# Attention tiled by head pairs and query halves, q and k in rows of 2 KB, v sums copied by DMA, and attention of batch 1 run before the experts

## The chip, the core and the metric

The kernel runs on one core of a Trainium2 chip. The time is device microseconds of one launch; the median of three runs stands for a kernel. The profile is one execution on the chip. Its engines are PE (matrix multiply, with PEld for its weight loads), DVE, ACT, POOL and SP; POOL and SP also issue the DMAs here (POOL those that load from DRAM and cast float32 to bf16, SP the rest).

## What is computed

Sparse attention over 4 batches, 8 heads, 768 positions of 64, followed by one expert (two matrix products) that is chosen for each batch from the mean over its positions. Cut to what matters:

```
k_sum = k.reshape(B, H, 24, 32, D).max(axis=3)      # 24 blocks of 32 keys
v_sum = v.reshape(B, H, 24, 32, D).mean(axis=3)
scores_l = scale * q @ k.T,  kept where |i - j| < 16, else -1e9
scores_s = scale * q @ k_sum.T + log(32)
a = softmax(concatenate([scores_l, scores_s]))
x = a @ concatenate([v, v_sum])                      # B, S, H * D = 512
e = argmax(x.mean(axis=1) @ w_gate)                  # one expert of 8 for each batch
out = gate_w * (relu(x @ w1[e]) @ w2[e])             # 512 -> 1024 -> 512
```

## The kernel before

Queries go in blocks of 64 (QB). A block's keys are 120 rows: its own 64, a halo of 16 on either side, and the 24 block maxima; `kaug` holds k transposed with these columns for each pair of heads and block, `vblk` the rows of v in the same order (own rows, halo rows R_PRE and R_POST, 24 rows of block sums). Four batches run one after another. Instructions are issued in the order in which the Python code calls them; nothing reorders them, and each engine works its own list in that order.

Loads: `load_k`, `load_q` (through `load_rows`, L83) issue six DMAs each, one for 128 positions of all heads, in rows of 256 bytes; `load_v` (L98) two DMAs, 256-byte rows too. All are in POOL's list. `halo` (L107) copies the halo rows of v inside `vblk` with SP DMAs once v has landed.

Attention of a batch: `T_k` (L191) transposes k on PE and copies it to `kaug`; `K_rest` (L206) adds halo columns and the maxima for the whole batch, on DVE; `V_sum` (L236) sums v by blocks on PE and copies the sums into `vblk` on DVE; then for each of six groups g of 128 queries, all heads at once: `T_q` (transpose q), `S_tile` (scores on PE, exponential on ACT, mask product on DVE), `O_tile` (product with v on PE, reciprocal and scaling on DVE), `X_tile` (transpose back on PE, copy on ACT, sum over positions on DVE, L346).

Expert of a batch: `gate` (L353) finds the expert and issues the six weight DMAs from POOL; `H_chunk` (L416) is one of 8 chunks of the first product, `O_chunk` (L438) half of one of six chunks of the second, with the scaling by the gate on ACT (L454) and an output DMA on SP (L455).

Order (L500 to L531): batch 0's attention alone; gate 0; loads of v and q of batch 1 behind the weights; k of batch 1; then `weave`, which puts steps of a second list between the items of a first: the first product of batch 0 with v and the first steps of q of batch 1, the second product with batch 1's S, O and X steps; and so on. After batch 3's gate, the rest of batch 2's second product and batch 3's expert run alone.

Of the kernel before, what the change touches and what calls it, by code (L numbers as in the profile page):

```python
# [22 lines left out]
def kernel(  # L23
# [71 lines left out]
    def load_q(b):
        load_rows(b, "q", q)

    def load_v(b):  # L98
        vb = vblks[b % NV]
        for a in range(2):  # L100
            hs = slice(4 * a, 4 * a + 4)
            nc.gpsimd.dma_start(  # L102
                vb[0:QB, hs, :, 0:D].rearrange("p h j d -> p (h j) d"),
                v[b, hs].rearrange("h (j p) d -> p (h j) d", p=QB),
            )

    def halo(b):  # L107
        vb = vblks[b % NV]
        for a in range(2):
            hs = slice(4 * a, 4 * a + 4)  # L110
            nc.sync.dma_start(
                vb[R_PRE : R_PRE + HALO, hs, 1:NJ, :],
                vb[QB - HALO : QB, hs, 0 : NJ - 1, :],
            )
            nc.sync.dma_start(
                vb[R_POST : R_POST + HALO, hs, 0 : NJ - 1, :], vb[0:HALO, hs, 1:NJ, :]
            )


    load_k(0)  # L120
    identb = const.tile([128, 128], BF16, name="identb")
    make_identity(nc, identb)
    it_u = const.tile([R_SUM, QB], I32, name="it_u")
    nc.gpsimd.iota(it_u, pattern=[[-1, QB]], base=0, channel_multiplier=1)
    it_p = const.tile([128, 1], I32, name="it_p")
    nc.gpsimd.iota(it_p, pattern=[[0, 1]], base=0, channel_multiplier=1)
    it_b = const.tile([QB, NJ, BLK], I32, name="it_b")
    nc.gpsimd.iota(it_b, pattern=[[-2, NJ], [1, BLK]], base=0, channel_multiplier=0)
    load_v(0)
    load_q(0)  # L130

# [3 lines left out]
    def edges(i):  # L135

        nc.vector.memset(vblks[i][0:QB, :, :, D:DP], 1.0)
        nc.vector.memset(vblks[i][QB:R_SUM, :, 0:1, :], 0.0)
# [34 lines left out]
    u_f = const.tile([R_SUM, QB], FP32, name="u_f")  # L173
    nc.vector.tensor_scalar(
        out=u_f, in0=it_u, scalar1=lo[:, 0:1], scalar2=None, op0=ALU.subtract
    )
    u_hi = const.tile([R_SUM, QB], FP32, name="u_hi")
    nc.vector.tensor_scalar(
        out=u_hi, in0=u_f, scalar1=float(2 * HALO - 2), scalar2=None, op0=ALU.is_le
    )  # L180
    mask = const.tile([NR, QB], BF16, name="mask")
    nc.vector.memset(mask[R_SUM:NR, :], 1.0)
    nc.vector.scalar_tensor_tensor(
        out=mask[0:R_SUM, :], in0=u_f, scalar=0.0, in1=u_hi, op0=ALU.is_ge, op1=ALU.mult
    )
    mask_b = mask.unsqueeze(1).to_broadcast([NR, 2 * H, QB])
# [4 lines left out]
    def T_k(b, gg):  # L191
        def f():
            k_nat = nat["k", b]
            ps = tps_pool.tile([128, NP, 2, 128], BF16, name="kps", tag="tps")
            for u in range(2):
                for pr in range(NP):
                    nc.tensor.transpose(  # L197
                        ps[:, pr, u, :], k_nat[:, 2 * gg + u, 2 * pr : 2 * pr + 2, :], identb
                    )
            nc.vector.tensor_copy(  # L200
                kaugs[b % 2][:, :, 4 * gg : 4 * gg + 4, 0:QB],
                ps.rearrange("p r u (t s) -> p r (u t) s", s=QB),
            )
        return f

    def K_rest(b):  # L206
        def f():
            ka = kaugs[b % 2]
            nc.vector.tensor_copy(
                ka[:, :, 1:NJ, R_PRE:R_POST], ka[:, :, 0 : NJ - 1, QB - HALO : QB]  # L210
            )
# [9 lines left out]
            cur = t1.rearrange("p n t s -> p (n t) s")  # L221
            while w > 1:
                w //= 2
                nxt = small.tile([128, NP * NB, w], BF16, name=f"t_{w}")
                nc.vector.tensor_tensor(
                    out=nxt, in0=cur[:, :, 0:w], in1=cur[:, :, w : 2 * w], op=ALU.max
                )
                cur = nxt
            kmx = cur.rearrange("p (r n) o -> p r (n o)", r=NP)
            nc.vector.tensor_copy(  # L230
                ka[:, :, :, R_SUM:NR],
                kmx.unsqueeze(2).to_broadcast([128, NP, NJ, NB]),
            )
# [101 lines left out]
    def X_tile(b, g):  # L335
        def f():
# [5 lines left out]
            for pr in range(NP):  # L342
                nc.tensor.transpose(xps[:, pr, 0, :], xs[:, pr, :, :], identb)  # L343
# [218 lines left out]
```

## Time and profile before

| | before |
|---|---|
| runs, us | 230.15, 228.45, 230.1 (median 230.1) |
| profiled execution, us | 228.99 |
| its span, us | 227.3 |
| PE busy | 151.1 us, 66% |
| DVE busy | 103.5 us, 46% |
| ACT busy | 81.8 us, 36% |
| POOL busy (mostly DMA issue) | 72.5 us, 32% |
| DMA packets | 92,578, of which 76,176 under 512 bytes |

The profiled execution's own time is 1.7 us longer than its span. A busy share is an average over stages with different limits; the stages are told apart by windows of the trace. The column PEclk of a window is the clock that the throttle granted to PE, as a share of full speed. A row `start us, us, what` of the chain of work that ended last says what the end of the program hung on at that time.

### The profile page before, as it was taken

Reading aid. Unit: us, or ns where it says so; the run is one execution under the profiler, and the core shown is the slowest. Engines: PE = TensorE matmul, PEld = TensorE weight load, DVE = VectorE, ACT = ScalarE, POOL = GpSimd, SP = SyncE. Lnnn points to the kernel's source line nnn. Section 1 sums busy time; section 2 is a strip of 40 time slices with the busy share of each in tenths; the row PEclk is TensorE's granted clock in tenths of the full one; section 3 lists DMA queues with packets and bytes.
Section 4 is the critical chain, followed back from the end, with each engine's and each line's share of the span. In section 5 each row is a group of like instructions: output and inputs, shape, how many; then the busy total and the mean of one; then the engine's idle time right before and its main releaser. Section 6 shows DMA issues by size and latency. Waiting matters only on the chain.

```text
span 227.3 us, 4141 instructions
## 1 busy us (share of the span) xinstructions
PE 151.1 (66%) x1721; PEld 90.8 (40%) x1736; DVE 103.5 (46%) x240; ACT 81.8 (36%) x113; POOL 72.5 (32%) x89
## 2 busy tenths in 40 slices
PE   0324596456029999822933999950899984999991
PEld 0213474432025555511612555520566552456440
DVE  2685689681006066750360626771167797100000
ACT  2000365102002666630420266650155684155441
POOL 7996100099335000009834684005100000520000
PEclk9999999999656999995895599995599999699998
DMA  7999990089999912219999999997990111399342
GB/s 46 120 135 140 138 50 0 0 105 194 166 133 140 118 46 95 92 50 111 185 168 134 139 136 149 200 198 109 152 169 0 49 49 46 41 185 237 66 165 94
DMA packets 92578, 25.88 MB, mean 114 GB/s; under 512 B 76176, under 2 KB 89488, under 8 KB 92560
## 3 DMA queue, kind: packets, MB, share of 16 engines
q0 software_dynamic: 87296, 17.83, 129.3%
q1 hardware_dynamic: 5264, 7.80, 12.8%
q8 instruction: 13, 0.21, 0.4%
q14 instruction: 5, 0.04, 0.1%
HBM read 35.67 MB, written 6.29 MB: 185 GB/s over the span
## 4 chain that ended last, share of the span: by engine, by line
PE 30%; DMA 29%; DVE 15%; ACT 8%; issue 8%; POOL 6%; POOLq 2%; SPq 0%; ACTq 0%
DMA vblk<-in_v_dram 18%; PE hps L424 12%; PE ops L445 11%; DMA w_sb<-in_moe_w_dram 8%; DVE aT L300 4%; DVE xs L327 4%; ACT aT L294 4%; DMA vblk<-vblk 4%; DVE red L346 3%; ACT o_sb L454 2%; POOL k_nat L87 2%; POOL vblk L102 2%; PE vsps L243 2%; PE ops L316 2%; POOL w_sb L383 1%
## 5 line engine op out<-in xcount | busy, mean ns | idle before, releaser
L424 PE MATMUL hps<-xT,w_sb 128*128 128x384 bf16 x256 | 54.2, 371 | 15.0 <-DMA w_sb<-in_moe_w_dram 14.9
L431 ACT ACTIVATE hT<-hps 128x768 bf16<-128x768 f32 x32 | 26.0, 811 | 72.0 <-PE hps L424 72.0
L445 PE MATMUL ops<-w_sb,hT 128*128 128x512 bf16 x177 | 47.0, 391 | 2.4 <-issue 0.8
L383 POOL DMA_DIRECT2D w_sb<-in_moe_w_dram x16 | 11.9, 758 | 104.1 <-DVE grec L397 82.4
L424 PEld LDWEIGHTS <-w_sb 128*128 128x128 bf16 x256 | 26.8, 109 | 35.4 <-DMA w_sb<-in_moe_w_dram 15.7
L294 ACT ACTIVATE aT<-sc 128x1024 bf16<-128x1024 f32 x24 | 24.5, 1021 | 26.7 <-PE sc L284 26.6
L87 POOL DMA_DIRECT2D k_nat<-in_k_dram x24 | 21.3, 898 | 14.5 <-DMA vblk<-in_v_dram 11.7
L300 DVE TENSOR_TENSOR aT<-aT,mask 120x1024 bf16<-120x1024 bf16 x24 | 16.6, 690 | 20.3 <-ACT aT L294 20.2
L445 PEld LDWEIGHTS <-hT 128*128 128x128 bf16 x192 | 17.3, 99 | 18.6 <-issue 2.9
L87 POOL DMA_DIRECT2D q_nat<-in_q_dram x24 | 21.4, 927 | 7.6 <-DMA w_sb<-in_moe_w_dram 6.6
L454 ACT ACTIVATE o_sb<-ops,gcol 128x512 f32<-128x512 f32 x24 | 16.5, 687 | 18.7 <-PE ops L445 17.0
L243 PE MATMUL vsps<-vblk,bind 64*32 64x132 bf16 x192 | 6.2, 286 | 24.3 <-DMA vblk<-in_v_dram 24.3
L345 ACT COPY xT<-xps 128x512 bf16<-128x512 bf16 x24 | 14.0, 585 | 13.8 <-PE xps L343 13.6
L200 DVE COPY kaug<-kps 128x1024 bf16<-128x1024 bf16 x12 | 8.1, 687 | 22.0 <-PE kps L197 22.0
L346 DVE TENSOR_REDUCE red<-xT 128x4 f32<-128x512 bf16 x24 | 16.3, 682 | 3.6 <-ACT xT L345 3.6
L327 DVE TENSOR_TENSOR xs<-ops,rv 128x512 bf16<-128x512 f32 x24 | 16.6, 692 | 0.8
L197 PE MATMUL kps<-identb,k_nat 128*128 128x128 bf16 x96 | 10.1, 275 | 10.1 <-POOL identb masks.py:199 7.4
L243 PEld LDWEIGHTS <-bind 64*32 64x32 bf16 x192 | 4.9, 126 | 26.3 <-issue 21.8
L316 PE MATMUL ops<-vblk,aT 120*64 120x65 bf16 x384 | 12.1, 210 | 3.9 <-DVE aT L300 1.6
L343 PE MATMUL xps<-identb,xs 128*128 128x128 bf16 x96 | 10.7, 241 | 4.5 <-DVE xs L327 4.5
L197 PEld LDWEIGHTS <-k_nat 128*128 128x128 bf16 x96 | 8.8, 127 | 11.5 <-DMA k_nat<-in_k_dram 5.5
L251 DVE CAST vs_sb<-vsps 128x132 bf16<-128x132 f32 x4 | 1.2, 293 | 26.5 <-PE vsps L243 26.5
(58 smaller groups left out, 132.8 us busy)
## 6 DMA issues: line engine op xcount, KB each, us to landing
out_dram<-o_sb SPq DMA_DIRECT2D x24, 256.0 KB, 2.0
w_sb<-in_moe_w_dram POOLq DMA_DIRECT2D x16, 256.0 KB, 6.4
w_sb<-in_moe_w_dram POOLq DMA_DIRECT2D x8, 512.0 KB, 10.6
k_nat<-in_k_dram POOLq DMA_DIRECT2D x24, 128.0 KB, 9.6
vblk<-in_v_dram POOLq DMA_DIRECT2D x8, 384.0 KB, 13.4
q_nat<-in_q_dram POOLq DMA_DIRECT2D x24, 128.0 KB, 13.4
vblk<-vblk SPq DMA_DIRECT2D x16, 90.8 KB, 8.4
wg_sb<-in_moe_w_gate_dram SPq DMA_DIRECT2D x1, 16.0 KB, 1.9
```

The source lines that it names most:

```text
L87: nc.gpsimd.dma_start(t[:, g, :, :], src[b, :, g * 128 : (g + 1) * 128, :].rearrange("h p d -> p h d"),)
L197: nc.tensor.transpose(ps[:, pr, u, :], k_nat[:, 2 * gg + u, 2 * pr : 2 * pr + 2, :], identb)
L243: nc.tensor.matmul(vs_ps[BLK * pr : BLK * (pr + 1), :], lhsT=bind[:, j, :], rhs=vb[0:QB, 2 * pr : 2 * pr + 2, j, :], start=(j == 0), stop= ...
L294: nc.scalar.activation(aT.rearrange("p n c -> p (n c)"), sc.rearrange("p h c -> p (h c)"), ACT.Exp, scale=SCALE,)
L300: nc.vector.tensor_tensor(out=aT[0:NR], in0=aT[0:NR], in1=mask_b, op=ALU.mult)
L316: nc.tensor.matmul(ops[w * QB : (w + 1) * QB, hh, pr, :], lhsT=aT[0:NR, hh, pr, w, :], rhs=vb[0:NR, 2 * pr + hh, 2 * g + w, 0 : D + 1], st ...
L327: nc.vector.tensor_tensor(out=xs.rearrange("p r h d -> p h r d"), in0=ops[:, :, :, 0:D], in1=rv.unsqueeze(3).to_broadcast([128, 2, NP, D]) ...
L346: nc.vector.tensor_reduce(out=red[b][:, :, g], in_=dst, axis=AX.X, op=ALU.add)
L424: nc.tensor.matmul(hps[:, half, 0:HB], lhsT=w1_sb[:, dt, ft * 128 : (ft + 1) * 128], rhs=xT[b][:, dt, half * HB : (half + 1) * HB], start= ...
L431: nc.scalar.activation(hTs[b][:, ft, :].rearrange("p (u s) -> p u s", u=2), hps[:, :, 0:HB], ACT.Relu,)
L445: nc.tensor.matmul(o_ps, lhsT=hTs[b][:, ft, st * 128 : (st + 1) * 128], rhs=w2_sb[:, ft, :], start=(ft == 0), stop=(ft == NFT - 1),)
L454: nc.scalar.activation(o_sb, o_ps, ACT.Copy, scale=gcols[b][:, 0:1])
```

## The change

q and k are loaded as `[96, heads, 512]`: eight neighbouring positions of a head lie in one partition, so a row of DRAM is 2 KB (512 float32) and a batch needs one DMA for k and one for q. In batch 0 the loads go pair of heads by pair of heads: k, v, q of heads 0 and 1, then of 2 and 3, and so on. The transposes are now 16 for each pair, 96 columns each, and the copies behind them (`T_k`, `T_q`) read PSUM with a step of 96 elements to bring positions back in order. q's copy is on ACT in batch 0.

Attention goes by pair of heads and half of the queries (u), six blocks of 64 each. `T_k` does all of a pair's columns: copy, two maxima, one reduce, halo columns, block maxima. The mask is added on PE in batch 0 (`mbias` times `ident6`, two matmuls of 384 columns for each S_tile) and multiplied on DVE in the others. The sum over positions comes from ACT's `accum_out` in `X_tile`. The copies of v's block sums into `vblk` are DMAs on SP, two for each pair, and the halos of batch 0 are issued by pair. Odd output chunks are scaled on DVE.

PSUM is cut into one score buffer of two banks, two for transposes and four single banks for all else. `H_chunk` is one half of the queries, so there are 16 of them.

Order: batch 0's attention, with batch 1's loads and masks in its middle; gate 0; the first 19 of 33 steps of batch 1's attention alone; then 9 H items of batch 0 woven with the other 14 steps; gate 1; 19 items of batch 0 with 22 of batch 2's 33 steps; 9 of batch 1 with the rest; gate 2; the same for batch 3; gate 3; the rest of batch 2; batch 3's expert. Weights of batch 0 come in five DMAs for w1, of the others in three, and two for w2.

```
+        nc.gpsimd.dma_start(
+            nat[which, b][:, h0:h1, :],
+            src[b, h0:h1].rearrange("h (p r) d -> p h (r d)", r=RR),
+        )
...
+    def transpose_pair(b, which, pr, name):
+        src = nat[which, b]
+        ps = tps_pool.tile([128, RR, PR], BF16, name=name, tag="tps")
+        for r in range(RR):
+            for hh in range(2):
+                nc.tensor.transpose(
+                    ps[hh * D : (hh + 1) * D, r, :],
+                    src[:, 2 * pr + hh, r * D : (r + 1) * D],
+                    identb[0:PR, 0:PR],
+                )
+        return ps
...
+    def T_k(b, pr):
+        def f():
+            ps = transpose_pair(b, "k", pr, "kps")
+            ka = kaugs[b % 2][:, pr]
             nc.vector.tensor_copy(
+                ka[:, :, 0:QB].rearrange("q j (p r) -> q j p r", r=RR),
+                ps.rearrange("q r (j p) -> q j p r", j=NJ),
+            )
...
+            nc.vector.tensor_reduce(
+                out=kmx, in_=t2.rearrange("p j t s -> p (j t) s"), axis=AX.X, op=ALU.max
+            )
...
+    def V_sum(b, prs):
...
+            for pr in prs:
+                for hh in range(2):
+                    nc.sync.dma_start(
+                        vb[R_SUM:NR, 2 * pr + hh, :, 0:D],
+                        vs_sb[BLK * pr : BLK * pr + NB, hh, :]
+                        .unsqueeze(1)
+                        .to_broadcast([NB, NJ, D]),
+                    )
...
+            nc.scalar.activation(
+                xT[b][:, pr, u * HB : (u + 1) * HB], xps, ACT.Copy,
+                accum_out=red[b][:, pr, u : u + 1],
+            )
...
+        for pr in range(p0, p1):
+            ahead = pre(pr + 1) if pr + 1 < NP else []
+            nq = [T_q(b, pr + 1)] if pr + 1 < NP else []
+            steps += [S_tile(b, pr, 0)]
+            steps += ahead[0:1]
+            steps += [S_tile(b, pr, 1)]
+            steps += ahead[1:]
+            steps += [O_tile(b, pr, 0), O_tile(b, pr, 1)]
+            steps += nq
+            steps += [X_tile(b, pr, 0), X_tile(b, pr, 1)]
...
+    a0 = attn(0, 0, NP)
+    run(a0[: len(a0) // 2])
     load_k(1)
     edges(1)
+    make_mask()
+    load_v(1, 0, 4)
+    load_v(1, 4, 8)
+    load_q(1)
+    run(a0[len(a0) // 2 :])
     gate(0)
     load_k(2)
+    a1 = attn(1, 0, NP)
+    n1 = len(attn(1, 0, 2))
+    run(a1[:n1])
+    m0, m1, m2, m3 = moe(0), moe(1), moe(2), moe(3)
+    weave(m0[0:9], a1[n1:])
...
+    weave(m0[9:28], a2[: 2 * len(a2) // 3])
+    weave(m1[0:9], a2[2 * len(a2) // 3 :])
...
+    weave(m1[9:28], a3[: 2 * len(a3) // 3])
+    weave(m2[0:9], a3[2 * len(a3) // 3 :])
     gate(3)
+    run(m2[9:])
+    run(m3)
```

POOL's list at the start of the program, before: k of batch 0 in six DMAs, the identity matrix and the index tables, v, q, k of batch 1, then what the gate waits for.

```order
L87 DMA k_nat<-in_k_dram 128x8x64 x6
masks.py:197 MEMSET identb 128x128
masks.py:199 ISA
masks.py:199 AFFINE_SELECT identb<-identb 128x128
L124 IOTA it_u 96x64
L126 IOTA it_p 128x1
L128 IOTA it_b 64x384
L102 DMA vblk_84<-in_v_dram 64x48x64 x2
L87 DMA q_nat<-in_q_dram 128x8x64 x6
L87 DMA k_nat<-in_k_dram 128x8x64 x6
L370 TENSOR_LOAD ix_601
```

The same place in the changed kernel, to the second pair's loads.

```order
L91 DMA k_nat<-in_k_dram 96x2x512
masks.py:197 MEMSET identb 128x128
masks.py:199 ISA
masks.py:199 AFFINE_SELECT identb<-identb 128x128
L104 DMA vblk_87<-in_v_dram 64x24x64
L91 DMA q_nat<-in_q_dram 96x2x512
L127 IOTA it_b 64x384
L129 IOTA it_p 128x1
L132 IOTA it_m 128x64
L133 IOTA it_m 128x16
L136 IOTA it_m 128x16
L91 DMA k_nat<-in_k_dram 96x2x512
```

The identity and the tables moved from behind six loads to behind one, and v and q of the first pair stand ahead of k of the second. Batch 1's loads now stand ahead of the gate's `TENSOR_LOAD`.

SP's list at the start, before: the gate weights, then the halo copies of batches 0 and 1 (two groups of four), then outputs.

```order
L133 DMA wg_sb<-in_moe_w_gate_dram 128x4x8
L111 DMA vblk_84<-vblk_84 16x4x726
L115 DMA vblk_84<-vblk_84 16x4x726
L111 DMA vblk_84<-vblk_84 16x4x726
L115 DMA vblk_84<-vblk_84 16x4x726
```

The same place in the changed kernel: for each pair two halos and two copies of block sums (`vs_sb`).

```order
L150 DMA wg_sb<-in_moe_w_gate_dram 128x4x8
L111 DMA vblk_87<-vblk_87 16x2x726
L115 DMA vblk_87<-vblk_87 16x2x726
L306 DMA vblk_87<-vs_sb 24x12x64 x2
L111 DMA vblk_87<-vblk_87 16x2x726
L115 DMA vblk_87<-vblk_87 16x2x726
L306 DMA vblk_87<-vs_sb 24x12x64 x2
```

The copies of block sums moved from DVE to this queue; a later pair's halo stands behind an earlier pair's copies.

ACT's list behind gate 0 (its exponential is `ex`), before: all eight chunks of batch 0's first product, then batch 1's first scores (`aT`) among the outputs.

```order
L393 ACTIVATE ex_624,se<-lg,negm 1x8
L431 ACTIVATE hT<-hps 128x768 x8
L294 ACTIVATE aT<-sc 128x1024
L454 ACTIVATE o_sb<-ops_866,gcol 128x512
L294 ACTIVATE aT<-sc 128x1024 x2
```

The same place in the changed kernel.

```order
L449 ACTIVATE ex_784,se<-lg,negm 1x8
L357 ACTIVATE aT<-sc 128x768 x2
L400 ACTIVATE xT,red<-xps 128x384 x2
L357 ACTIVATE aT<-sc 128x768 x2
L400 ACTIVATE xT,red<-xps 128x384 x2
L484 ACTIVATE hT<-hps 128x384
L357 ACTIVATE aT<-sc 128x768
L484 ACTIVATE hT<-hps 128x384
```

Two pairs of batch 1's attention (scores and transposes back) moved ahead of the first `hT`.

## Rows read from the trace of the kernel before

**Rows 1.** Windows by stage: stretch, length, busy us (count) by engine, PEclk, DMA, GB/s.

```profile
0.00:28.00 28.00, 8.38 (x132) 6.84 (x133) 16.39 (x40) 3.33 (x3) 20.05 (x29) 1.00 2.47 115
28.00:41.60 13.60, 10.19 (x188) 7.41 (x183) 11.61 (x24) 7.49 (x10) 0.00 (x0) 1.00 0.51 25
41.60:68.40 26.80, 10.69 (x99) 7.00 (x100) 8.34 (x26) 2.01 (x4) 14.62 (x17) 0.81 1.92 128
68.40:97.60 29.20, 27.41 (x327) 15.53 (x331) 16.67 (x33) 16.81 (x23) 3.13 (x4) 0.94 1.06 95
97.60:124.80 27.20, 11.97 (x125) 7.64 (x126) 7.72 (x21) 5.53 (x10) 14.73 (x17) 0.78 1.85 134
124.80:151.80 27.00, 24.96 (x309) 14.15 (x314) 16.78 (x34) 14.90 (x20) 11.10 (x12) 0.91 2.74 163
151.80:159.80 8.00, 0.37 (x9) 0.26 (x8) 2.24 (x9) 0.98 (x4) 4.04 (x6) 0.61 0.78 129
159.80:193.40 33.60, 28.52 (x399) 18.03 (x402) 22.84 (x48) 17.69 (x23) 0.43 (x1) 0.94 0.41 76
193.40:227.30 33.90, 28.61 (x144) 13.97 (x146) 0.90 (x7) 13.07 (x19) 4.45 (x6) 0.92 0.63 132
```

**Rows 2.** The chain that ended last: start us, us, what, count.

```profile
9.33 9.13 DMA vblk<-in_v_dram
...
19.11 8.66 DMA vblk<-vblk
...
51.38 15.44 DMA vblk<-in_v_dram
...
72.96 2.60 PE hps L424 x16
...
78.38 0.34 PE sc L284 x16
...
84.37 0.44 PE ops L316 x16
...
165.00 0.45 PE kps L197 x8
...
169.79 0.80 PE vsps L243 x48
...
213.03 9.67 PE ops L445 x44
```

**Rows 3.** Timeline, batch 0: start us, us, engine, line, instruction, count, idle before.

```profile
11.07 1.28 DVE L200 COPY kaug<-kps 128x1024 bf16<-128x1024 bf16 x2
...
23.94 0.61 PE L284 MATMUL sc<-qT,kaug 64*128 64x64 bf16 x16 [2.97 <-DVE qT L271]
```

**Rows 4.** Groups by line and shape: busy us, mean ns of one, idle before.

```profile
L431 ACT ACTIVATE hT<-hps 128x768 bf16<-128x768 f32 x32 | 26.0, 811 | 72.0 <-PE hps L424 72.0
...
L327 DVE TENSOR_TENSOR xs<-ops,rv 128x512 bf16<-128x512 f32 x24 | 16.6, 692 | 0.8
L300 DVE TENSOR_TENSOR aT<-aT,mask 120x1024 bf16<-120x1024 bf16 x24 | 16.6, 690 | 20.3 <-ACT aT L294 20.2
...
L346 DVE TENSOR_REDUCE red<-xT 128x4 f32<-128x512 bf16 x24 | 16.3, 682 | 3.6 <-ACT xT L345 3.6
...
L271 DVE COPY qT<-qps 128x512 bf16<-128x512 bf16 x24 | 9.9, 419 | 5.8 <-PE qps L266 5.7
...
L200 DVE COPY kaug<-kps 128x1024 bf16<-128x1024 bf16 x12 | 8.1, 687 | 22.0 <-PE kps L197 22.0
...
L209 DVE COPY kaug<-kaug 128x704 bf16<-128x704 bf16 x4 | 1.9, 468 | 0.1
...
L225 DVE TENSOR_TENSOR t<-t 128x384 bf16<-128x384 bf16 x4 | 1.4, 358 | 0.1
```

**Rows 5.** Time from issue to landing: halo copies of L111, then outputs of L455.

```profile
DMA to landing us min/median/max: 2.6/7.4/9.0
...
DMA to landing us min/median/max: 2.0/2.0/7.1
```

More of the change, by code (lines that the diff above doesn't have):

```diff
@@ L107, in halo, with load_rows @@
-    def halo(b):
-        vb = vblks[b % NV]
[L109 to L120, printed above, removed]
+    def load_rows(b, which, src, h0, h1):
+        if (which, b) not in nat:
+            nat[which, b] = ld.tile([PR, H, RR * D], BF16, name=f"{which}_nat")
+        nc.gpsimd.dma_start(
+            nat[which, b][:, h0:h1, :],
+            src[b, h0:h1].rearrange("h (p r) d -> p h (r d)", r=RR),
+        )
@@ L127 @@
[L127 to L130, printed above, removed]
+    for pr in range(2, NP):
+        load_k(0, 2 * pr, 2 * pr + 2)
+        load_v(0, 2 * pr, 2 * pr + 2)
+        load_q(0, 2 * pr, 2 * pr + 2)
     wg_sb = const.tile([128, NDT, E], FP32, name="wg_sb")
@@ L180 @@
     )
[L181 to L184, printed above, removed]
-    )
-    mask_b = mask.unsqueeze(1).to_broadcast([NR, 2 * H, QB])
-    xT, red, qTs, xss, aTs = {}, {}, {}, {}, {}
-    def T_k(b, gg):
-        def f():
[L193 to L199, printed above, removed]
+    nc.vector.tensor_tensor(out=d_f, in0=d_f, in1=d_f, op=ALU.mult)
@@ new lines, in f @@
+            qT = qTs[b, pr]
+            on_pe = b == 0
+            sc = sc_pool.tile([128, 2, 512], FP32, name="sc", tag="sc")
+            if on_pe:
+                for hh in range(2):
+                    rs = slice(hh * D, (hh + 1) * D)
+                    nc.tensor.matmul(
+                        sc[:, hh, 0:HB],
+                        lhsT=mbias[rs, :],
+                        rhs=ident6[rs].rearrange("p w c -> p (w c)"),
+                        start=True,
+                        stop=False,
+                        tile_position=(hh * D, 0),
+                    )
@@ new lines, in f @@
+            for w in range(NW):
+                for hh in range(2):
+                    rs = slice(hh * D, (hh + 1) * D)
+                    j = u * NW + w
+                    nc.tensor.matmul(
+                        sc[:, hh, w * QB : (w + 1) * QB],
+                        lhsT=ka[rs, pr, j, :],
+                        rhs=qT[rs, j * QB : (j + 1) * QB],
+                        start=not on_pe,
+                        stop=not on_pe or w == NW - 1,
+                        tile_position=(hh * D, 0),
+                    )
@@ L303, in S_tile, with O_tile @@
+            aT = work.tile([128, 2, HB], BF16, name="aT")
+            aTs[b, pr, u] = aT
+            nc.scalar.activation(aT, sc[:, :, 0:HB], ACT.Exp, scale=SCALE)
+            if not on_pe:
+                av = aT[0:NR].rearrange("p h (w c) -> p (h w) c", c=QB)
+                nc.vector.tensor_tensor(out=av, in0=av, in1=masks[0], op=ALU.mult)
         return f
-    def O_tile(b, g):
+    def O_tile(b, pr, u):
         def f():
             vb = vblks[b % NV]
-            aT = aTs.pop((b, g)).rearrange("p (h r w) c -> p h r w c", h=2, w=2)
-            ops_raw = big_pool.tile([128, 2, 512], FP32, name="ops", tag="big")
-            ops = ops_raw[:, :, 0 : NP * (D + 1)].rearrange(
-                "p h (r c) -> p h r c", c=D + 1
-            )
-            for hh in range(2):
-                for pr in range(NP):
+            aT = aTs.pop((b, pr, u))
+            ops = one_pool.tile([128, NW // 2, 2, D + 1], FP32, name="ops", tag="one")
+            for t in range(NW // 2):
+                for hh in range(2):
@@ L353, in gate @@
     def gate(b):
[L354 to L357 removed]
+        lgps = one_pool.tile([128, 512], FP32, name="lgps", tag="one")
+        for i in range(2 * NP):
             nc.tensor.matmul(
                 lgps[0:1, 0:E],
[L360 to L363 removed]
+                lhsT=red[b][:, i // 2, i % 2 : i % 2 + 1],
+                rhs=wg_sb[:, i // 2, :],
+                start=(i == 0),
+                stop=(i == 2 * NP - 1),
             )
```

425 lines of the change are left out of this document (203 added, 222 removed).

## The prediction

> **What bounds the kernel now.** I read the stage table first (busy time by stretch), then the chain of work that ended last, then single rows for prices. The stage table [rows 1] shows a program that is held by PE only in parts. In the woven stretches (68.4 to 97.6, 124.8 to 151.8, 159.8 to 193.4) and in the last one, PE is busy 84 to 94% of the time. Between them lie four stretches in which it is not: up to 28.0 us PE has 8.38 us of work, since it waits for batch 0's loads; from 41.6 to 68.4 and from 97.6 to 124.8 it has 10.7 and 12.0 us of work in 27 us; from 151.8 to 159.8 it has 0.37 in 8.0. The chain names the cause: v of batch 0 is waited for from 9.33 for 9.13 us and its halo copy lands 8.66 us after its issue at 19.11, and v of batch 1 is waited for over 15.44 us because it was queued behind the expert's weights [rows 2]; batch 2 repeats that. The 8.0 us are the gate and the first weight chunk with no other work ready. So about 20 + 16 + 15 + 8 = 59 us of 227.3 are PE waiting for something that could have been fetched or computed sooner. The last stage runs at PE's pace: 44 matmuls in 9.67 us, ending at 222.7, and 4.6 us of output behind them.
>
> **What stays.** The experts' PE work is unchanged. At the faster pace, 16 matmuls of 384 columns take 2.60 us (0.163 each) and 44 of 512 take 9.67 (0.22 each) [rows 2]. A half chunk H is 4 x 0.163 = 0.65 us, half an O chunk 4 x 0.22 = 0.88. A batch has 16 H and 12 O items: 21.0 us.
>
> **Attention by pairs, PE.** Each pair has 32 transposes of 96 columns (8 of 128 took 0.45: 0.042 each, 1.35), 24 scores (16 took 0.34: 0.51), 24 outputs (16 took 0.44: 0.66) and 6 transposes back (0.34) [rows 2]: 2.86 us. Four pairs and 48 v sums (0.80) are 12.2 us for a batch.
>
> **Attention by pairs, DVE.** T_k is now seven instructions for each pair. The first maximum has a row of its own size (384 elements in 0.358); by the slopes of the rows beside it the second is about 0.26, the halo columns 0.2 each (704 elements took 0.468), the reduce of 192 elements 0.35 (512 took 0.682) and the copy of 288 some 0.23 [rows 4]. The copy out of PSUM is not in the trace: 768 elements read with a step of 96. Contiguous, 1024 took 0.687 and 512 took 0.419, so 0.55 for 768. One element at a time, as `xs` goes (512 in 0.692), it is 0.95 [rows 4]. I take 0.95, because the elements read one after another are no longer neighbours, as in the f32 row. T_k is then 2.5 us for each pair, T_q 0.95, the mask 0.55 (1024 in 0.690), both O tiles 1.5, so 6.1 us a pair with both masks; a batch is 25 us, and batch 0, whose mask is on PE and whose q copy is on ACT, 17. [...] What leaves DVE is the pooling reduce (24 x 0.682) and the v-sum copies; half the output scalings come to it. DVE ends near 110 us of work, against the 103.5 that the stretches sum to: no bound over the program, but one where attention runs alone.
>
> **Batch 0.** Rows of 2 KB make k and q cheap; loads come pair by pair, so PE starts on pair 0 while the rest arrives. The constants on DVE, behind which the first k copy started at 11.07 [rows 3], follow one load instead of six on POOL, so I put that copy at 8, the first scores at 11. The first outputs need the v-sum rows. These were DVE copies and are now two SP DMAs behind the halos, issued near 12. The nearest row is the halo on the same queue: 2.6 to 9.0 us to land, 7.4 in the middle [rows 5], long when loads are queued, as they are here. So the first O tile is at 20, not at 27.8. After that a pair is the larger of two things. PE: 4.2 us at the faster pace (2.86, 0.65 for the mask's four wide matmuls, 0.67 for 12 v sums that go one by one). The trace has 16 scores in 0.61 in batch 0 against 0.34 later [rows 2, 3], a factor of 1.8, although the clock column reads 1.00 there; so 7.6 at the slower pace. DVE and its handover: 2.5 + 0.3 + 1.5 and 1.7 of PE and semaphores around it, 6.0. I take 6.8. Three periods and 2 us for the end: 20 + 20.4 + 2 = 42 us, bounds 34 (landing in 2.6, period 6) and 49 (landing in 9.0, period 7.6, and edges and masks of batch 1 in DVE's way). Before, this point was 41.6: the earlier start is eaten by the pair's chain.
>
> **Batch 1's first half, alone.** Its loads were queued right behind batch 0's and have landed; the weights of batch 0 land behind it, and that wait is hidden. DVE sets the pace: 5.5 us until the first scores, then 8.2 a pair (6.1, and 2.1 in which DVE waits for scores, the exponential of 0.81 [rows 4] and the transposes), 2 us for a v-sum DMA that lands late: 24 us. Bounds 18 (DVE without gaps) and 29. 42 + 24 = 66.
>
> **The five woven stretches.** They hold 28 items of batch 0, 28 of batch 1 and 9 of batch 2: 47.8 us of PE; 4.4 of batch 1's attention and 12.2 each of batches 2 and 3: 28.8. Together 76.6. PE's busy share in such stretches was 85 to 94% [rows 1]; 90% makes 85.5, and I add 2 us for the first matmuls at the slow pace and 2 x 2 us for the v-sum DMAs of batches 2 and 3, which are issued while weights load, some 5 us ahead of their use: 92. Bounds 82 and 99. DVE's 25 us a batch and 2 for scalings stay below PE's 33.
>
> **The end.** What is left of batch 2 (7 H, 12 O) is 15.1 us and covers the gate and the weights of batch 3, for which PE stood still before; batch 3 is 21.0, the output 4.6: 40.7.
>
> **Sum.** 42 + 24 + 92 + 40.7 = 198.7 us of span. The profiled execution took 228.99 for a span of 227.3, so 1.7 more: 200. It lies within the three runs shown (228.45 to 230.15, median 230.1), 1.1 below the median; I leave that out.
>
> **Rivals.** *Everything lands early.* Halo and v-sum DMAs land in 2.6 as they do with no loads queued, and PE is granted the faster clock in batch 0: 34 + 20 + 84 + 40.7 + 1.7 = 180. For it: pairs keep PE fuller than it was in batch 0 (8.38 busy in 28 us). Against: loads are queued until some 33 us. *Late by a little everywhere.* The upper bounds of the stages: 49 + 29 + 99 + 41 + 1.7 = 220. *No gain.* The same with the weaving at 107, a PE share of 71%: 228; no stretch of the trace is that bad once its loads are there. *Slower than before.* A v-sum DMA has 288 short rows where a halo has 64. If landing with loads queued grows with the rows, 7.4 - 2.6 = 4.8 for 64 makes 21.6 for 288, 24 to land. The first O tile then comes 17 us later, batch 1 loses 17, and batches 2 and 3 each 8 (until their weights are in): 200 + 50 = 250. It decides once the landings cost 30 us in all, at about 17 each. Against it: output DMAs of 128 rows landed in at most 7.1 [rows 5], no longer than halos of 64. [...]
>
> **Chances.** Forecast, 188 to 212: 0.57. Early: 0.20. Late by a little: 0.15. No gain: 0.03. Slower: 0.05. So faster by over 1% 0.92, within 1% (what a measurement of this kernel can tell from no change) 0.03, slower 0.05. From the early and late cases I leave out the outer half each: 182 to 220.
>
> **What would show it.** Right: first O tile near 20 us, gate of batch 0 near 43, first H matmul near 66, no PE wait for v or weights after it, last H stage starting as batch 2 ends. The k copy near 0.95 us, not 0.55. Wrong: v-sum DMAs landing beyond 10 us, or PE idle over 15% of a woven stretch with DVE full, which would make DVE the bound.

## The result, and the profile of the changed kernel

The changed kernel takes 219.5 us (median of 4 runs, 218.9 to 223.0) against 229.3 us before: a ratio of 0.957, 95% interval 0.951 to 0.962. It is faster, as forecast, but by 10 us and not by 30; 219.5 lies just inside the upper end of the range. The rows below are from a second measurement of the same kernel (221.5 us, span 220.1), so that they share their chip with the first experiments. All that follows adds up in spans; the time outside it is 1.8 us here and 1.7 before.

First the windows by stage, which answer to [rows 1]: stretch, length, busy us (count) of PE, PEld, DVE, ACT, POOL, then PEclk, DMA share, GB/s. The boundaries are the first O tile, gate 0, the first H matmul, gate 1, the change from batch 0's items to batch 1's, gate 2, the same change, gate 3.

```profile
0.00:21.00 21.00, 7.87 (x125) 6.31 (x127) 9.94 (x35) 3.70 (x4) 15.04 (x28) 1.00 1.36 137
21.00:47.90 26.90, 18.61 (x309) 14.03 (x307) 13.19 (x47) 11.61 (x25) 0.00 (x0) 1.00 1.61 110
47.90:70.10 22.20, 11.49 (x252) 9.43 (x253) 15.80 (x43) 5.29 (x12) 9.47 (x11) 1.00 1.17 151
70.10:85.80 15.70, 13.52 (x196) 7.64 (x194) 7.94 (x20) 9.62 (x23) 0.00 (x0) 1.00 2.04 117
85.80:122.50 36.70, 29.09 (x387) 15.44 (x390) 19.47 (x50) 12.72 (x27) 8.00 (x9) 0.86 1.47 172
122.50:134.00 11.50, 9.05 (x134) 5.46 (x134) 6.27 (x18) 7.04 (x18) 0.00 (x0) 1.00 0.22 43
134.00:168.50 34.50, 27.91 (x386) 14.92 (x388) 19.59 (x51) 12.84 (x28) 3.74 (x5) 0.90 0.61 117
168.50:179.70 11.20, 8.91 (x133) 5.46 (x134) 6.01 (x17) 6.92 (x18) 0.00 (x0) 1.00 0.01 2
179.70:220.10 40.40, 36.45 (x190) 18.61 (x190) 5.54 (x14) 15.62 (x31) 3.71 (x5) 1.00 0.57 130
```

The long waits for loads that [rows 1] showed are gone: no stretch has PE below 50% except the first 21 us, where the loads arrive. But the woven stretches, which had PE at 84 to 94%, have it at 79 to 86%. The chain of work that ended last says why (start us, us, what), where [rows 2] had waits for `in_v_dram`:

```profile
16.52 10.78 DMA vblk<-vs_sb
28.40 10.34 DMA vblk<-vs_sb
52.81 6.94 DMA vblk<-vs_sb
90.56 10.02 DMA vblk<-vs_sb
138.75 8.80 DMA vblk<-vs_sb
```

Five landings of the small copies of v's block sums are 46.9 us, 21% of the span: two in batch 0 and one in each of batches 1 to 3. What PE waited for (engine line, releaser: us, times, longest):

```profile
PE ops L372 <- DMA vblk<-vs_sb: 22.8, 9, 5.0
PE ops L372 <- DVE aT L360: 7.7, 7, 2.2
```

The place in the program, behind gate 1 (timeline: start us, us, engine, line, instruction, count, idle before):

```profile
87.72 2.26 POOL L439 DMA_DIRECT2D w_sb<-in_moe_w_dram  x3 [28.04 <-DVE grec L453]
89.68 12.62 SPq L306 DMA_DIRECT2D vblk<-vs_sb  x8
92.18 2.76 POOL L104 DMA_DIRECT2D vblk<-in_v_dram  x2
98.64 0.27 PE L372 MATMUL ops<-vblk,aT 120*64 120x65 bf16 x2 [4.45 <-DMA vblk<-vs_sb]
100.62 0.82 PE L372 MATMUL ops<-vblk,aT 120*64 120x65 bf16 x22 [1.71 <-DMA vblk<-vs_sb]
104.48 1.89 PE L498 MATMUL o_ps<-w_sb,hT 128*128 128x512 bf16 x4
108.21 1.03 PE L498 MATMUL o_ps<-w_sb,hT 128*128 128x512 bf16 x4
```

Eight copies are issued from 89.68, two microseconds behind the first weights of batch 1 and just ahead of k, v and q of batch 3. PE comes to the first O tile at 94.2, 4.5 us later, and PE can't pass it, since its list is in order: it stands 4.45 and 1.71 us. Then it is slow, too: four O matmuls take 1.89 us at 104.48 and 1.03 at 108.21. The granted clock in windows of PE alone (stretch, length, busy, PEclk, DMA share, GB/s):

```profile
92.00:94.00 2.00, 2.00 (x36) 1.00 0.75 86
96.00:98.00 2.00, 0.00 (x0) 0.91 1.38 209
98.00:100.00 2.00, 0.27 (x2) 0.50 1.39 213
104.00:106.00 2.00, 2.00 (x18) 0.50 1.53 207
106.00:108.00 2.00, 2.00 (x8) 0.53 2.53 143
108.00:112.00 4.00, 3.95 (x53) 1.00 4.08 135
```

The clock fell while PE stood, at about 97.6 (0.91 from 96 to 98), and stayed at 0.50 until about 107.9 (0.53 from 106 to 108); before the wait it was 1.00. A wait of 6 us thus costs more than 6.

Durations, by line and shape (busy us, mean ns | idle before), against [rows 4]:

```profile
L258 DVE COPY kaug<-kps 128x768 bf16<-128x768 bf16 x16 | 15.2, 951 | 5.7 <-PE kps L241 5.7
L252 DVE COPY qT<-qps 128x768 bf16<-128x768 bf16 x12 | 11.4, 952 | 4.7 <-PE qps L241 4.6
L360 DVE TENSOR_TENSOR aT<-aT,mask 120x768 bf16<-120x768 bf16 x24 | 13.3, 556 | 24.3 <-ACT aT L357 24.3
L276 DVE COPY kaug<-kaug 128x176 bf16<-128x176 bf16 x16 | 5.3, 330 | 0.0
```

The copies out of PSUM with a step take 0.95 us, as the forecast took them.

### The profile page after: what moved, and what is told of

It is laid out like the page before. It is cut to its first block, busy times and chain, and to the rows that moved or that the text cites. A ratio compares the mean times of both kernels' runs of the same rounds, so it can differ in the third digit from the quotient of the medians.

```text
span 221.2 us, 5022 instructions
## 1 busy us (share of the span) xinstructions
PE 164.1 (74%) x2094; PEld 97.8 (44%) x2104; DVE 103.8 (47%) x292; ACT 85.5 (39%) x185; POOL 40.0 (18%) x58
## 3 DMA queue, kind: packets, MB, share of 16 engines
q0 software_dynamic: 42720, 17.83, 83.9%
## 4 chain that ended last, share of the span: by engine, by line
PE 44%; DMA 20%; DVE 17%; ACT 11%; issue 3%; POOL 2%; SPq 1%; ACTq 0%; POOLq 0%; DVEq 0%
DMA vblk<-vs_sb 20%; PE o_ps L498 18%; PE hps L477 12%; ACT aT L357 4%; DVE kaug L258 4%; PE ops L372 4%; ACT xT L400 3%; PE qps L241 3%; DVE aT L360 2%; PE xps L399 2%; PE sc L347 2%; DVE t L265 2%; ACT hT L484 1%; DVE kmx L273 1%; SPq L306 1%
## 5 line engine op out<-in xcount | busy, mean ns | idle before, releaser
L498 PE MATMUL o_ps<-w_sb,hT 128*128 128x512 bf16 x182 | 49.2, 408 | 0.6 <-issue 0.4
L484 ACT ACTIVATE hT<-hps 128x384 bf16<-128x384 f32 x64 | 31.4, 491 | 24.3 <-PE hps L477 24.3
L439 POOL DMA_DIRECT2D w_sb<-in_moe_w_dram x14 | 10.5, 760 | 144.0 <-PE hps L477 84.4
L357 ACT ACTIVATE aT<-sc 128x768 bf16<-128x768 f32 x32 | 26.0, 812 | 15.2 <-PE sc L347 14.2
L372 PEld LDWEIGHTS <-aT 120*64 120x64 bf16 x384 | 10.9, 132 | 40.9 <-issue 18.2
L360 DVE TENSOR_TENSOR aT<-aT,mask 120x768 bf16<-120x768 bf16 x24 | 13.3, 556 | 24.4 <-ACT aT L357 24.4
L400 ACT ACTIVATE xT<-xps 128x384 bf16<-128x384 bf16 x32 | 15.6, 490 | 21.8 <-PE xps L399 21.5
L383 DVE TENSOR_TENSOR xs<-ops,rv 128x384 bf16<-128x384 f32 x32 | 17.8, 558 | 1.1
L258 DVE COPY kaug<-kps 128x768 bf16<-128x768 bf16 x16 | 15.2, 952 | 5.8 <-PE kps L241 5.8
L347 PE MATMUL sc<-qT,kaug 64*128 64x64 bf16 x384 | 13.4, 210 | 5.3 <-DVE qT L252 2.6
L347 PEld LDWEIGHTS <-kaug 64*128 64x128 bf16 x384 | 10.8, 107 | 12.8 <-issue 10.1
L241 PE MATMUL kps<-identb,k_nat 96*64 96x96 bf16 x256 | 11.1, 245 | 5.0 <-POOL it_p L129 5.0
L252 DVE COPY qT<-qps 128x768 bf16<-128x768 bf16 x12 | 11.4, 952 | 4.7 <-PE qps L241 4.6
```

Of the source, the lines that this page charges most:

```text
L241: nc.tensor.transpose(ps[hh * D : (hh + 1) * D, r, :], src[:, 2 * pr + hh, r * D : (r + 1) * D], identb[0:PR, 0:PR],)
L258: nc.vector.tensor_copy(ka[:, :, 0:QB].rearrange("q j (p r) -> q j p r", r=RR), ps.rearrange("q r (j p) -> q j p r", j=NJ),)
L347: nc.tensor.matmul(sc[:, hh, w * QB : (w + 1) * QB], lhsT=ka[rs, pr, j, :], rhs=qT[rs, j * QB : (j + 1) * QB], start=not on_pe, stop=not o ...
L357: nc.scalar.activation(aT, sc[:, :, 0:HB], ACT.Exp, scale=SCALE)
L360: nc.vector.tensor_tensor(out=av, in0=av, in1=masks[0], op=ALU.mult)
L372: nc.tensor.matmul(ops[w * QB : (w + 1) * QB, t, hh, :], lhsT=aT[0:NR, hh, c0 : c0 + QB], rhs=vb[0:NR, 2 * pr + hh, u * NW + 2 * t + w, 0 ...
```

## The experiments

Each kernel was measured beside the kernel before. The stages, us from the start of the profiled execution; the forecast's in the first line:

| kernel | median, us | ratio and interval | gate 0 | first H | gate 1 | gate 2 | gate 3 | span |
|---|---|---|---|---|---|---|---|---|
| forecast | 200 | | 42 | 66 | | | 158 | 198.7 |
| changed, again | 221.5 | 0.967 (0.961 to 0.973) | 47.9 | 70.1 | 85.8 | 134.0 | 179.7 | 220.1 |
| sums on DVE | 207.3 | 0.904 (0.899 to 0.909) | 40.1 | 63.1 | 78.9 | 122.1 | 165.7 | 206.6 |
| sums early | 207.1 | 0.905 (0.898 to 0.912) | 47.4 | 67.7 | 85.3 | 126.2 | 165.1 | 205.5 |
| one set of weights | 210.0 | one run | 46.1 | 67.7 | 83.0 | 128.2 | 167.8 | 208.2 |
| half the rows | 209.8 | one run | 44.7 | 66.7 | 82.2 | 125.4 | 167.8 | 208.2 |
| both | 201.3 | 0.885 (0.880 to 0.890) | 40.1 | 59.5 | 77.9 | 118.8 | 157.8 | 198.2 |
| k behind outputs | 198.9 | 0.874 (0.869 to 0.879) | 40.6 | 60.7 | 77.4 | 116.6 | 154.6 | 195.0 |
| plain copies | 195.7 | 0.855 (0.850 to 0.861) | 39.5 | 57.5 | 77.3 | 116.1 | 153.5 | 193.9 |
| no head start | 232.9 | 1.021 (1.012 to 1.030) | 46.0 | 51.2 | 94.0 | 142.9 | 190.6 | 231.0 |
| q on ACT | 198.4 | 0.871 (0.862 to 0.879) | 40.7 | 58.9 | 77.4 | 118.2 | 155.2 | 195.6 |
| late outputs | 194.1 | 0.843 (0.836 to 0.850) | 40.4 | 55.8 | 79.0 | 116.7 | 152.0 | 192.4 |
| v ahead of k | 192.7 | 0.837 (0.831 to 0.844) | 40.9 | 58.9 | 75.0 | 114.3 | 151.3 | 191.7 |

### The changed kernel again

No edit; it is the base of the comparisons.

> The changed kernel once more, for a second profile and beside the others: 219 us by both theories. In its profile PE waits for block-sum copies four to six times, 3 to 6 us each.

221.5 us; its profile is shown above.

### The sums on DVE

The copies of block sums go back from SP's queue to DVE, one for each pair:

```
-                for hh in range(2):
-                    nc.sync.dma_start(
-                        vb[R_SUM:NR, 2 * pr + hh, :, 0:D],
-                        vs_sb[BLK * pr : BLK * pr + NB, hh, :]
-                        .unsqueeze(1).to_broadcast([NB, NJ, D]))
+                nc.vector.tensor_copy(
+                    vb[R_SUM:NR, 2 * pr : 2 * pr + 2, :, 0:D],
+                    vs_sb[BLK * pr : BLK * pr + NB, :, :]
+                    .unsqueeze(2).to_broadcast([NB, 2, NJ, D]))
```

> One part undone: the block sums of v go into vblk by DVE copies (0.57 us a pair before) instead of SP DMAs. Theory L (what the forecast missed is that these DMAs land 7 to 10 us after their issue): the waits of 9, 9, 7, 10 and 9.5 us on the chain go, and the slow PE clock behind two of them; DVE gets 9 us more work. 196 to 201 us. Theory D (DVE and its handovers set the pace of attention in any case, the waits only lie beside it): 212 to 218 us.

207.3 us: 14 us faster, though DVE does 16 copies of 0.67 us more. It lies between the two theories' ranges: gate 0 comes 7.8 us sooner, but the five woven stretches only fall from 109.6 to 102.6 us, with the copies now among DVE's work. Batch 0 shows the landings best. O tiles of the changed kernel:

```profile
19.75 0.27 PE L372 MATMUL ops<-vblk,aT 120*64 120x65 bf16 x2 [5.04 <-DMA vblk<-vs_sb]
27.01 1.15 PE L372 MATMUL ops<-vblk,aT 120*64 120x65 bf16 x24
37.14 0.27 PE L372 MATMUL ops<-vblk,aT 120*64 120x65 bf16 x2 [3.04 <-DMA vblk<-vs_sb]
38.78 0.82 PE L372 MATMUL ops<-vblk,aT 120*64 120x65 bf16 x22 [1.37 <-DMA vblk<-vs_sb]
```

and with the sums on DVE:

```profile
15.51 0.87 PE L371 MATMUL ops<-vblk,aT 120*64 120x65 bf16 x24 [0.55 <-DMA vblk<-vblk]
22.93 0.87 PE L371 MATMUL ops<-vblk,aT 120*64 120x65 bf16 x24
29.95 0.87 PE L371 MATMUL ops<-vblk,aT 120*64 120x65 bf16 x24
36.30 0.54 PE L371 MATMUL ops<-vblk,aT 120*64 120x65 bf16 x12
```

Two landings cost batch 0 7.8 us (gate 0 at 47.9 and 40.1): one at its first O tile, one in the third pair's. Without them the period of a pair is (36.30 - 15.51) / 3 = 6.9 us.

### The sums early

`V_sum` of batches 1 to 3 is called one stretch earlier, and v is loaded for it in time; the copies stay DMAs:

```
-            if b > 0:
-                steps.append(V_sum(b, list(range(NP))))
...
+    run(a0[len(a0) // 2 : -4])
+    V_sum(1, allp)()
+    run(a0[-4:])
     gate(0)
     load_k(2)
+    load_v(2, 0, 4)
+    load_v(2, 4, 8)
...
+    weave(m0[0:9], t1[0:7] + [V_sum(2, allp)] + t1[7:])
```

(and batch 3 likewise.)

> The copies stay DMAs, but the v sums of batches 1, 2 and 3 are computed and issued one stretch earlier (batch 1's ahead of batch 0's last outputs, 2's and 3's inside the stretch before their own). Theory L: no wait for them in batches 1 to 3, batch 0 as before: 219 less about 5, 8 and 8, 196 to 202 us. Theory D: 212 to 218 us.

207.1 us, above the 196 to 202 of theory L and below the 212 to 218 of theory D. Batch 0 is as before, with its two landings in the chain; the others are gone from it:

```profile
10.64 9.32 DMA vblk<-vs_sb
28.02 9.12 DMA vblk<-vs_sb
```

Gate 1 to gate 2 goes from 48.2 to 40.9, gate 2 to gate 3 from 45.7 to 38.9: 7.3 and 6.8 us for the two late landings, wait and slow clock together (some 0.8 of the 6.8 are the sums' own matmuls, which moved a stretch ahead). Issued early, the copies also stand ahead of the next weights: those of batches 1 to 3 land 2.2 to 4.7 us behind their issue, by the semaphore updates in the trace. Windows from first H to gate 3 of this kernel, where no landing is in the way, and the longest of PE's waits in them:

```profile
67.70:85.30 17.60, 14.89 (x243) 8.69 (x242) 8.32 (x22) 9.79 (x23) 0.00 (x0) 1.00 1.88 127
85.30:126.20 40.90, 35.25 (x519) 19.23 (x523) 25.87 (x68) 20.10 (x45) 8.00 (x9) 1.00 1.14 167
126.20:165.10 38.90, 34.28 (x471) 18.68 (x475) 24.98 (x66) 19.77 (x45) 3.74 (x5) 1.00 0.49 98
PE ops L372 <- DVE aT L360: 6.0, 8, 1.4
```

### One set of weights, and half the rows

Two ways to ask why a landing takes 9 to 10 us. The first leaves out the weight loads of batches 1 to 3 (they compute with batch 0's expert):

```
+        if b > 0:
+            wts[b] = wts[0]
+        else:
+            load_w(b, e_val)
```

> Leaves out the weight loads of batches 1 to 3, which use batch 0's expert. If the block sums land late because weights load at the same time, they land within 4 us of issue in batches 2 and 3 and the stretches there lose their 6 us stalls: 203 us, with no change up to the first expert. If a copy of 288 short rows takes 9 us by itself: 217 to 219 us.

The second gives each DMA 144 rows of 128 bytes where it had 288, and the other half to DVE:

```
-                        vb[R_SUM:NR, 2 * pr + hh, :, 0:D],
+                        vb[R_SUM:NR, 2 * pr + hh, 0:NW, 0:D],
```

> The changed kernel, but each block-sum DMA writes the first six blocks only (144 rows instead of 288) and DVE copies the other six. If the landing under load grows with the number of rows, the waits of 9 to 10 us shrink to some 5 and the time to 207 to 211 us. If it is a fixed delay behind the queued loads: 217 to 222 us.

Both kernels take 210 us, in one run each. With one set of weights, batch 2's landing is still in the chain, with k, v and q of batch 3 queued then; batch 3's is not, and nothing is loaded then:

```profile
50.99 6.32 DMA vblk<-vs_sb
88.23 7.51 DMA vblk<-vs_sb
```

Batch 3's eight copies are issued from 132.06, with a DMA share of 0.00 from 128.2 to 132.0. By the semaphore updates in the trace each lands 2.2 to 2.3 us behind its issue, 288 rows and all, and PE comes to the first O tile without a wait (timeline):

```profile
136.50 0.38 PE L372 MATMUL ops<-vblk,aT 120*64 120x65 bf16 x12
```

With half the rows:

```profile
10.85 8.70 DMA vblk<-vs_sb
27.60 7.93 DMA vblk<-vs_sb
130.24 7.44 DMA vblk<-vs_sb
```

So it is the queued loads that make a landing late: the same copy takes 2.2 us with nothing queued, 7.5 with k, v and q queued and 10.0 with the weights too. A copy of 288 rows doesn't take 9 us by itself. While loads are queued, its own rows count as well. With half of them the copy at 27.60 in batch 0 lands in 7.9 us, where that copy took 9.1 to 10.3 in five profiles that have it whole; batch 3's takes 7.4, against 8.8 and 9.5 in the changed kernel's two profiles. But landing is far from proportional to rows: half of them save an eighth to a quarter. What PE waits for these copies falls more, from 22.8 to 9.1 us, since the wait is only what is left of a landing.

### Both, and k behind the outputs

Batch 0's sums go by DVE, the others' early by DMA; then, on top, the next pair's `T_k` stands behind both outputs in batches 1 to 3:

```
-            steps += [S_tile(b, pr, 0)] + ahead[0:1] + [S_tile(b, pr, 1)]
-            steps += [O_tile(b, pr, 0), O_tile(b, pr, 1)]
+            steps += [S_tile(b, pr, 0), S_tile(b, pr, 1)]
+            steps += [O_tile(b, pr, 0), O_tile(b, pr, 1)]
+            steps += ahead
```

> The two cures together: batch 0's block sums by DVE copies, those of batches 1 to 3 by DMAs issued a stretch early. Theory L (late landings are what the forecast missed): the first gate at 40 as with DVE copies (48 in the changed kernel), and every later stretch as with early sums, so 207 less 7: 200 us (198 to 203).

> As the run with both cures, but in batches 1 to 3 the next pair's T_k stands behind both outputs instead of between the two score tiles. Theory C (what is left of the miss is DVE's order: T_k's seven instructions, 2.5 us, stand between a pair's two masks and hold its second output): the woven stretches lose 1 us and more for each pair, 190 to 195 us against about 200. Theory P (PE sets the pace there): within 3 us of the run with both cures.

201.3 and 198.9 us. Each way alone gave 14 us, both together 19 (ratios 0.967 to 0.885): they overlap in batches 1 to 3. The order of k is worth 2.4 us, within what theory P allowed and less than theory C had; the woven stretches alone fall from 98.3 to 93.9. Both have a new wait, 0.6 and 0.4 us: v of batch 2 is now wanted in the first woven stretch, and its load stands behind the weights and k:

```profile
49.89 19.95 DMA vblk<-in_v_dram
```

### Plain copies

"Both", with k and q copied out of PSUM in the order in which they lie there, positions left permuted, to price the step of 96 elements by itself:

```
-                ka[:, :, 0:QB].rearrange("q j (p r) -> q j p r", r=RR),
-                ps.rearrange("q r (j p) -> q j p r", j=NJ),
+                ka[:, :, 0:QB],
+                ps.rearrange("q r p -> q (r p)").rearrange("q (j c) -> q j c", c=QB),
```

> As the run with both cures, but the copies of k and q out of PSUM go in the order in which the elements lie (leaves out putting positions back in order). Price: 0.55 us instead of 0.95 for each copy of 768 elements. Theory C: these copies lie on the chain, 4 to 7 us less than with both cures. Theory P: 0 to 2 us less, from the stretches where attention runs alone.

```profile
L258 DVE COPY kaug<-kps 128x768 bf16<-128x768 bf16 x16 | 8.8, 550 | 5.1 <-PE kps L241 5.1
L252 DVE COPY qT<-qps 128x768 bf16<-128x768 bf16 x12 | 6.5, 541 | 2.6 <-PE qps L241 2.6
```

0.55 and 0.54 us each where they took 0.95: both of the forecast's two prices were right to the hundredth. The step costs 5.7 us of the median (201.3 to 195.7) and 4.3 of the profiled span (198.2 to 193.9), as theory C had it. Of the 4.3, the woven stretches give 2.3 (98.3 to 96.0).

### No head start

The changed kernel, with all of batch 1's attention woven into the first 9 H items:

```
-    n1 = len(attn(1, 0, 2))
+    n1 = 0
```

> The changed kernel without the head start of batch 1: none of batch 1's 33 attention steps runs ahead of the experts, all are woven with the first 9 H items of batch 0. In the changed kernel the stretch from gate 0 to gate 1 takes 22.2 + 15.7 = 37.9 us. Theory of the forecast (the head start hides the landing of batch 0's weights): PE now stands at the first H for some 8 us, as it did between 151.8 and 159.8 us in the kernel before, and then attention of batch 1 and 9 H items take what DVE needs, 25 us of work and some 5 of gaps: 38 us or a little more, so 0 to 5 us slower than the changed kernel (ratio to the kernel before 0.96 to 0.99). Rival: the weights land within 2 us of the gate, and nothing was hidden: 30 us, some 7 faster (ratio 0.93).

232.9 us, 11.4 slower than the changed kernel and 2% slower than the kernel before: more than either theory had. The wait for the weights is 5.2 us and not 8. What comes on top are waits in the woven stretch, the longest for block sums again:

```profile
PE ops L372 <- DMA vblk<-vs_sb: 6.0, 2, 4.2
PE hps L477 <- DMA w_sb<-in_moe_w_dram: 5.2, 1, 5.2
```

and that PE stays at its slow pace all along, with 31.4 us of work in 42.8: each of the nine H items takes 1.46 to 1.49 us there, where they took 1.48, 1.46 and seven times 0.82 in the changed kernel. So the head start is worth 10 us between gates 0 and 1 (48.0 against 37.9).

### q on ACT, late outputs, v ahead of k

Three steps from "k behind outputs": q's copy on ACT in all batches; on top of it, either each tile's outputs one tile later, or v of batch 2 loaded ahead of its k.

```
-                "act" if b == 0 else "dve",
+                "act",
```

> The fastest kernel so far (batch 0's block sums copied by DVE, the others' fetched one stretch earlier, next pair's k behind both outputs; 198.9 us) with the copy of q out of PSUM on ACT in every batch, not in batch 0 alone: 12 copies of 0.95 us leave DVE, 12 of 0.80 come to ACT. If DVE's chain of copies still sets the pace of the woven stretches, some 3 us are gained (195 to 197 us). If the pace is set by the handover from PE to ACT and back (scores, exponential of 0.81, outputs), the copies stand ahead of an exponential on ACT, and it is the same or up to 3 us slower (198 to 202).

198.4 us, the same. Of DVE's work 8 us leave the woven stretches between the first H and gate 3, and these take 96.3 us, where they took 93.9: DVE's work is not their bound, unless what came to ACT cost as much as DVE gained. The stretch of batch 1 alone gains 1.9 us (20.1 to 18.2), the next loses it.

```
+                steps += [S_tile(b, pr, 0)] + ahead
+                if pr > 0:
+                    steps += [O_tile(b, pr - 1, 1), X_tile(b, pr - 1, 0)]
+                steps += [S_tile(b, pr, 1)] + nq + [O_tile(b, pr, 0)]
...
```

> The kernel with q on ACT (198.4 us) with the outputs of a score tile issued behind the next pair's transposes or the next score tile, in batches 1 to 3, so that PE doesn't come to them while ACT and DVE still make their weights. In that kernel, PE is idle 1.7 of 18.4, 4.0 of 40.9 and 2.8 of 37.0 us in the woven stretches by its rows, and 8.6 of 17.9 in the first half of batch 1 that runs alone. If the handover PE, ACT, DVE, PE holds the alone stretch, it falls from 17.9 to some 13 us and the woven ones by 1 to 3 more: 191 to 194 us. Rival: DVE holds the alone stretch (12.2 us busy there), and the woven stretches are at PE's pace: 196 to 199, the same.

```
-    load_k(2)
     load_v(2, 0, 4)
     load_v(2, 4, 8)
+    load_k(2)
```

> The kernel with q on ACT (198.4 us) with v of batch 2 loaded ahead of k of batch 2. PE waits 1.7 us in the first woven stretch for v of batch 2 (and its sums then land behind). If that wait and the slow pace behind it (9 H items took 10.8 us there, against 9 x 0.82 = 7.4) are the load's doing, 2 to 4 us are gained: 194 to 196. If the slow pace there comes from what stood before (attention alone, PE half idle), only the wait goes: 196 to 198.

194.1 and 192.7 us; the second is better than either case of its expectation. With late outputs the stretch alone takes 15.4 us (18.2 before) and the last two woven ones 37.7 and 35.3 (40.8 and 37.0), PE at 93 and 96%; the first woven one grows from 18.5 to 23.2, for PE reaches V_sum(2) sooner and v is not there:

```profile
66.52 0.29 PE L294 MATMUL vsps<-vblk,bind 64*32 64x128 bf16 x2 [3.09 <-DMA vblk<-in_v_dram]
70.80 1.46 PE L294 MATMUL vsps<-vblk,bind 64*32 64x128 bf16 x46 [3.99 <-DMA vblk<-in_v_dram]
```

The 46 sums behind the wait take 1.46 us, where they took 0.84 with q on ACT behind a wait of 1.69:

```profile
68.94 0.84 PE L294 MATMUL vsps<-vblk,bind 64*32 64x128 bf16 x46 [1.69 <-DMA vblk<-in_v_dram]
```

With v ahead of k, PE doesn't wait for v in the first woven stretch at all (0.7 us remain in the next, for v of batch 3), and the stretch falls to 16.1; of its H items only the first two take 1.46 to 1.48 us, where with q on ACT two more did, at 70.97 and 72.80. This kernel is the fastest tried, a ratio of 0.837 to the kernel before and 13% below the changed one. The two edits together were not tried.

## Why the prediction was right in direction and wrong in size

The span is 21.4 us longer than forecast (220.1 against 198.7). By its own steps:

- **What was waited for before.** Right: the long waits for v and for weights, and those at the gates, are gone, with the rows above in place of [rows 1, 2]. POOL's queue moves 17.83 MB in 42,720 packets where it took 87,296 before; the time that these took, as a share of 16 engines' span, is 85.8% where it was 129.3%.
- **The prices of instructions.** Right: 0.95 us for the copies, 0.55 in plain order, DVE at 103.8 us of work against 110. The mark set for it ("near 0.95 us, not 0.55") is met.
- **First O tile at 20.** 19.75, by luck: the first copy was issued at 9.8 and not near 12, and landed after 9.9 us and not 7.4. The two errors cancel.
- **Period of 6.8 us per pair in batch 0.** Right as PE's and DVE's period, 6.9 with the sums on DVE; wrong as the kernel's. The forecast let a landing delay the first pair alone. The third pair's cost 4.4 us more (3.04 + 1.37), and gate 0 came at 47.9, not at 42. With the sums on DVE it comes at 40.1.
- **Batch 1's first half in 24 us.** 22.2. Its 2 us for a late landing were right: with the sums early it is 20.3. The head start is worth what it was put there for, 10 us by the run without it.
- **Five woven stretches in 92 us.** This is the step that failed: 109.6, 17.6 more. Two terms in it were too small. *The landings of batches 2 and 3, at 2 us each*, cost 7.3 and 6.8 (sums early against the changed kernel; 12.2 in all, since the first woven stretch then grows by 1.9). They were taken to land like a halo, 7.4 us in the middle [rows 5], and to be issued 5 us ahead. Issue was 4.5 us ahead in batch 2; the copies that PE waited for last landed 10.0 and 8.8 us behind their issue; and behind the wait PE's granted clock was 0.50 for some 10 us (four O matmuls in 1.89 us, against 1.03 at 1.00), which the forecast priced at nothing. *PE's work and share*: without those landings the five stretches still take 97.4 us, not 88. There PE is busy for 84.4 us (14.89 + 35.25 + 34.28) where the forecast had 76.6 and 2 for the slow pace, and idle for 13.0 where 90% left 8.9 (76.6 at 90% is 85.1, not the 85.5 it used). The 76.6 came from rows of 16 and 44 matmuls in a run [rows 2]; woven, four H matmuls take 0.82 us (0.76 until the next instruction starts) and not 0.65, and the first two items take 1.46 to 1.48. Most of the idle time is the handover from PE to ACT to DVE and back: 6.0 us of it are waits for DVE's mask product, 2.8 for its copy of q and 2.1 for ACT's exponential. The late outputs take part of it out: 40.8 to 37.7 and 37.0 to 35.3.
- **The end in 40.7.** 40.4.

In sum: 4.1 more by the first H matmul, 17.6 (8.2 for the landings beyond the 4 allowed, 9.4 for work and handover) in the woven stretches, 0.3 less at the end.

Of the rivals, the time is that of *late by a little everywhere* (220), but the profile is another: two stages are at or below the forecast, and the woven one is over its bound of 99, and over the 107 of *No gain* too, though PE's share in it was 81% (88.5 us of work in 109.6) and not 71%. That 219.5 lies inside the range is luck: the stages are 10.6 us over one bound and 8.5 under the other three, and the second measurement, 221.5, lies outside. *Slower than before* named the mechanism that was at work, copies of 288 short rows that land late while loads are queued, and priced it at 24 us of landing; on the chain it was 7 to 11, below the 17 at which it decides. The mark for wrong, "v-sum DMAs landing beyond 10 us", was met at 10.8, 10.3 and 10.0 us. The other was met by half: PE was idle for more than 15% of four of the woven stretches (21% from 85.8 to 122.5), but DVE was not full (19.47 us of 36.70). Its work was not the bound, as far as q on ACT tells, but the order of its work was in the way: k behind the outputs took 4.4 us from the woven stretches. With the landings off the path and k behind the outputs, the kernel takes what the change was forecast to give, 198.9 us.

## What to carry to other kernels

A small DMA between two engines' steps is not a cheap copy. The same copy that landed in 2.2 us with nothing queued took some 10 us among queued loads. So it is issued a whole stretch ahead of its use and ahead of the loads, or replaced by a copy on an engine. In a new kernel, look for such copies just behind the issue of a weight load; the row that gives them away is an engine that works in order and stands at the first instruction that needs the copy. A wait of PE is priced with what the clock takes behind it (here four O matmuls in 1.89 us instead of 1.03), and work that is woven in fours with the price of a four, not of a run (0.82 us for four H matmuls, not 0.65).

## What the runs showed of the hardware

- Copies of 288 rows of 128 bytes that the chain hung on took 8.8 to 10.8 us to land in the changed kernel while loads were queued (6.9 once), 144 rows 7.4 to 8.7; with nothing queued, 288 rows took 2.2 to 2.3 (one set of weights, batch 3). Those of one queue landed one behind another: of the eight issued from 89.68, the first landed at 98.50 and the next four 2.0 to 2.4 us apart, by the semaphore updates. SP was held by issuing them: eight took 12.62 us at 89.68, and 6.6 with nothing queued.
- In a wait of 4.45 us PE's granted clock fell, and it was 0.50 from about 97.6 to 107.9 us; four O matmuls took 1.89 us, against 1.03 once it was 1.00.
- The clock column reads 1.00 from 47.9 to 85.8 us in the changed kernel, but the first two H items take 1.48 and 1.46 us there and the others 0.82. The trace's first record of the clock is at 73.75, between the slow items and the fast (at 72.78 in the profile of the first measurement, behind items of 1.48 and 1.46 us and ahead of those of 0.82). Until then the column says nothing of the pace; the durations do.
- Copies of 176 elements within SBUF (L276) took 0.33 us in the mean, where the forecast had 0.2. Ten of the 16 took 0.20; the other six took 0.24 to 0.92 (0.24 at 89.01, 0.44 at 94.54), and each of these ran while POOL issued DMAs. That it is POOL's doing was not tried.
